# Moving the softmax's 1e-9 to GpSimd in ten units, with another opening order, one load of constants and a last product in two halves

## The chip, the core and the metric

The kernel runs on one core of one Trainium2 chip. A core has TensorE (PE, matrix products; its weight loads are listed as PEld), VectorE (DVE), ScalarE (ACT), GpSimd (POOL), and SyncE (SP), which here issues nearly all transfers. Each engine works through its own queue in order, and semaphores tie the queues together. The metric is the device time of one execution in microseconds.

## The reference

Eight batches of eight heads, 576 positions of 64 values. Heads 0 to 3 attend to the last 32 positions, heads 4 to 7 to every fourth of the last 128. The result, 4608 tokens of 512, goes through a layer with 1024 hidden values.

```python
scores = np.where(masks, scale * q @ k.T, -1e9)
attn = np.exp(scores - max(scores))
attn = attn / (np.sum(attn, axis=-1, keepdims=True) + 1e-09)
x = (attn @ v)                       # tokens x 512
h = x @ w_in                         # 512 -> 1024
e = np.exp(h - max(h)); sm = e / (sum(e) + 1e-9)
solu = h * sm
ln = (solu - mean(solu)) / np.sqrt(var(solu) + 1e-6) * g_ln
out = ln @ w_out                     # 1024 -> 512
```

The weights arrive as 64-bit floats and are turned into 32-bit ones on the chip. All products have 32-bit accuracy: each operand is split into a high and a low part, and three products of the parts are added.

## The kernel before, in words

There are 32 units (a batch and a pair of heads) and 36 tiles of 128 tokens. The order of every engine's queue is written out by hand: a list of words is run in order, and each word calls a function that issues its instructions to their engines. OPENING is the list for units 0 to 8 or so and tiles 0 to 5; STEP, PAIR and LAST_PAIR give the rest in loops.

A unit n goes through these words. `q` and `v` load its operands (lines 209, 210 and 217, on SP). `S` makes the scores on PE; in units 0 to 9 (PE_MASK) the mask is added by a product with the identity (line 247) ahead of the score products (line 255). `max` and `sub` find and subtract the maximum (DVE, lines 281 and 291; in the units of ACT_SCORES the scores are first copied out of PSUM by ACT, `cp`, line 285, and POOL subtracts, line 294). `exp` is ACT's (line 298), `sum` DVE's (line 302). `inv` adds 1e-9 and takes the reciprocal, both on DVE (lines 306 and 307). `norm` multiplies on POOL (line 312), `turn` transposes on DVE (line 317), `V` is the product with v on PE (line 333). `xh` and `xl` copy the result out as a high part (ACT, line 371) and a low part (DVE, line 388; in the units of POOL_X ACT makes a second copy, `xc`, line 375, and POOL subtracts, line 382).

The sixteen blocks of weights are loaded (`w`, line 232) and converted: `abs` and `low` on ACT (lines 780 and 790), `clamp`, `sign` and `join` on DVE (lines 796, 803 and 811), `gain` and `hi` on ACT (lines 818 and 821), `lo` on POOL, or on DVE for the blocks of DVE_LOW (line 825). In the first 88 us these fill the same queues as the softmax.

A tile i goes through `ha`, `hb`, `hc`, `hd` (a quarter each of the first product, line 401), `peak` (its row maximum, DVE, line 412), `e` (ACT, line 427), `gate` and `mid` (product, mean and centring, lines 436 to 445, with the centring on ACT in tiles 0 to 4), `var` (square and sum on ACT, line 452, then six small POOL operations that make rstd, lines 463 to 468), `forth` and `back` (through DRAM), `tr`, `th`, `tl` (transpose and split), `o` (the second product, line 531) and `out` (scaling and store, lines 544 to 555). Score and value products of a unit share PSUM banks with their neighbours: a unit's mask product waits until ACT or DVE has read the previous results there.

The last tile's output is scaled in two halves, by ACT (line 548) and DVE (line 551), into one tile, and each half is stored.

Of the kernel before, what the change touches and what calls it, by code (L numbers as in the profile page):

```python
# [130 lines left out]
def windowed_attention_then_solu_kernel(  # L131
# [7 lines left out]
    g_ln: bass.AP,  # L139
    mask: bass.AP,  # L140
    ident: bass.AP,
    ident_bf: bass.AP,
# [20 lines left out]
    id_sb = const.tile([P, P], F32, name="id_sb")  # L163
    mask_sb = const.tile([P, 2, NS * WQ], BF16, name="mask_sb")
    g_sb = const.tile([P, FT], F32, name="g_sb")
    id_bf = const.tile([P, P], BF16, name="id_bf")
# [137 lines left out]
    def soft_inv(n):  # L304
        rs = st[n]["rs"]
        nc.vector.tensor_scalar(out=rs, in0=rs, scalar1=1e-9, scalar2=None, op0=ALU.add)
        nc.vector.reciprocal(out=rs, in_=rs)
# [232 lines left out]
    def moe_out(i):  # L540
        ob = moe.tile([P, DO], F32, name="ob", bufs=1)
        rows, rstd = out[i * P : i * P + P, :], ms[i]["rstd"]
        if i < NTILE - 1:
            nc.scalar.activation(out=ob, in_=ps_o(i), func=AF.Copy, scale=rstd)  # L544
            nc.sync.dma_start(out=rows, in_=ob)
        else:
            left, right = slice(0, DO // 2), slice(DO // 2, DO)
            nc.scalar.activation(
                out=ob[:, left], in_=ps_o(i)[:, left], func=AF.Copy, scale=rstd
            )  # L550
            nc.vector.tensor_scalar(
                out=ob[:, right], in0=ps_o(i)[:, right], scalar1=rstd, scalar2=None, op0=ALU.mult
            )
            nc.scalar.dma_start(out=rows[:, left], in_=ob[:, left])
            nc.sync.dma_start(out=rows[:, right], in_=ob[:, right])
# [414 lines left out]
```

## Time and profile before

| what | value |
|---|---|
| runs | 501.33, 502.91, 503.94 us; median 502.91 |
| profiled execution | 504.69 us, of which the span of the trace is 502.8 |
| PE busy | 469.9 us (93%) |
| DVE, ACT, POOL busy | 351.4, 291.3, 298.7 us |
| transfers | 94.14 MB, mean 187 GB/s |

Busy time is the time in which an engine executes; a group's mean is that of one instruction. A wait is put down to what ended it. The chain of work that ended last is followed back from the last instruction, so it shows which engine set the end at each moment. "Issue" stands for idle time in which an engine waited for nothing that the profile shows. Times in the trace are counted from the start of the span.

### The profile page before, as it was taken

What the parts mean: (1) busy time and instruction counts of PE and PEld (TensorE: products, weight loads), DVE (VectorE), ACT (ScalarE), POOL (GpSimd) and SP (SyncE); (2) the same over time, 40 slices, a digit from 0 to 9 for tenths busy, and PEclk for the clock granted to TensorE, in tenths of its full rate; (3) what the DMA queues carried; (4) which work ended last, traced back from release to release, by engine and by line L of the source; (5) the groups of instructions that cost most, each with busy time, mean ns of one, the idle gap of its engine ahead of it and who ended that gap; (6) DMA issues with size and microseconds to landing.
All of it is one profiled execution on the core that took longest, in us unless ns stands there. A gap on an engine that the chain in (4) does not pass through costs nothing.

```text
span 502.8 us, 16542 instructions
## 1 busy us (share of the span) xinstructions
PE 469.9 (93%) x7064; PEld 376.0 (75%) x7064; DVE 351.4 (70%) x619; ACT 291.3 (58%) x483; POOL 298.7 (59%) x367
## 2 busy tenths in 40 slices
PE   1457998999999999999999999999999999999996
PEld 1336776788878888788878787878787888888875
DVE  3996989867627788777868686868676865445562
ACT  3766897744424444534457575757575767666551
POOL 1652776556533765778976666665756555766440
PEclk9999999999999999999999999999999999999999
DMA  7979175664465655666667677676765545354461
GB/s 280 402 254 359 37 261 163 230 190 133 137 193 156 194 164 169 186 175 178 201 175 216 206 211 211 210 211 211 212 210 164 160 129 146 104 168 124 113 188 63
DMA packets 51337, 94.14 MB, mean 187 GB/s; under 512 B 5952, under 2 KB 26048, under 8 KB 51264
## 3 DMA queue, kind: packets, MB, share of 16 engines
q1 hardware_dynamic: 50544, 92.43, 59.6%
q8 instruction: 55, 0.90, 0.8%
q10 hardware_dynamic: 720, 0.66, 0.4%
q14 instruction: 18, 0.15, 0.1%
HBM read 60.04 MB, written 28.31 MB: 176 GB/s over the span
## 4 chain that ended last, share of the span: by engine, by line
PE 91%; DMA 5%; issue 2%; DVE 1%; ACT 0%; SPq 0%; DVEq 0%; ACTq 0%
PE banks L531 40%; PE banks L733 20%; PE banks L401 18%; PE banks L333 7%; PE banks L255 6%; DMA qt<-qT 2%; DMA raw<-w_in 2%; DMA kt<-kT 1%; DVE pt L317 0%; PE banks L247 0%; DVE x_lo L388 0%; DVE nmax L412 0%; SPq L232 0%; DVE rs L302 0%; ACT sm L285 0%
## 5 line engine op out<-in xcount | busy, mean ns | idle before, releaser
L531 PE MATMUL banks<-w_o,th 128*128 128x512 f32 x576 | 179.9, 393 | 0.0
L522 POOL TENSOR_TENSOR tl<-t,th 128x512 fp32r<-128x512 f32 x68 | 87.9, 1305 | 59.9 <-ACT th L516 59.8
L531 PEld LDWEIGHTS banks<-w_o,th 128*128 128x128 f32 x576 | 106.6, 188 | 22.6 <-ACT th L516 0.6
L531 PE MATMUL banks<-w_o,tl 128*128 128x512 f32 x288 | 112.5, 391 | 0.0
L401 PE MATMUL banks<-w_i,x_hi 128*128 128x512 f32 x256 | 82.8, 405 | 0.2 <-DVE mu L436 0.2
L531 PEld LDWEIGHTS banks<-w_o,tl 128*128 128x128 f32 x288 | 54.0, 188 | 12.3 <-DVE tl L522 0.9
L516 ACT CAST th<-t 128x512 fp32r<-128x512 f32 x72 | 43.4, 621 | 23.5 <-DVE t L508 16.1
L401 PEld LDWEIGHTS banks<-w_i,x_hi 128*128 128x128 f32 x256 | 47.2, 191 | 11.1 <-DVE mu L436 0.8
L508 DVE STREAM_TRANSPOSE t<-raw 128x512 f32<-128x512 f32 x72 | 46.9, 684 | 6.1 <-DMA out<-ob 3.0
L401 PE MATMUL banks<-w_i,x_lo 128*128 128x512 f32 x128 | 50.7, 396 | 0.0
L333 PEld LDWEIGHTS banks<-pt,vt 32*64 32x64 f32 x2816 | 35.3, 138 | 20.0 <-issue 12.8
L452 ACT ACTIVATE e<-t 128x1024 f32<-128x1024 f32 x35 | 37.0, 1058 | 17.6 <-DVE t L448 17.3
L294 POOL TENSOR_TENSOR sm<-sm,mx 128x640 f32<-128x640 f32 x27 | 34.5, 1276 | 21.4 <-DVE mx L281 18.8
L333 PE MATMUL banks<-pt,vt 32*64 32x64 f32 (+3 forms) x2816 | 38.8, 234 | 8.6 <-issue 5.4
L298 ACT ACTIVATE sm<-sm 128x640 f32<-128x640 f32 x32 | 23.6, 739 | 35.8 <-POOL sm L294 35.1
L255 PEld LDWEIGHTS banks<-kt,qt 64*32 64x32 f32 x2560 | 29.8, 112 | 17.7 <-issue 10.7
L269 DVE TENSOR_TENSOR sm<-banks,mask_sb 128x640 f32<-128x640 f32 x22 | 18.1, 824 | 35.1 <-PE banks L255 35.0
L255 PE MATMUL banks<-kt,qt 64*32 64x64 f32 x2560 | 35.7, 238 | 5.6 <-issue 4.1
L544 ACT ACTIVATE ob<-banks,rstd 128x512 f32<-128x512 f32 x35 | 24.0, 686 | 24.8 <-issue 16.6
L757 DVE CUSTOM_DVE_ANT_0 t<-banks,t 128x512 f32<-128x512 f32 x30 | 20.7, 690 | 22.3 <-PE banks L733 16.9
L751 ACT COPY t<-banks 128x512 f32<-128x512 f32 x30 | 17.6, 588 | 30.3 <-PE banks L733 30.3
L427 ACT ACTIVATE e<-t,nmax 128x1024 f32<-128x1024 f32 x19 | 21.9, 1153 | 18.8 <-DVE nmax L764 18.2
(151 smaller groups left out, 868.5 us busy)
## 6 DMA issues: line engine op xcount, KB each, us to landing
mid<-t SPq DMA_DIRECT2D x140, 128.0 KB, 2.4
raw<-mid SPq DMA_DIRECT2D x34, 512.0 KB, 3.9
vt<-vw SPq DMA_DIRECT2D x32, 384.0 KB, 3.9
kt<-kT SPq DMA_DIRECT2D x32, 312.0 KB, 4.4
qt<-qT SPq DMA_DIRECT2D x32, 296.0 KB, 4.7
out<-ob SPq DMA_DIRECT2D x35, 256.0 KB, 2.7
x_hi<-x SPq DMA_DIRECT2D x12, 288.0 KB, 3.5
t<-w_in SPq DMA_DIRECT2D x5, 512.0 KB, 7.8
```

What stands on the lines that cost most here:

```text
L255: nc.tensor.matmul(out=ps[WIN * c : WIN * c + WIN, h, WQ * i : WQ * i + WQ], lhsT=qt[D * h : D * h + D, q0 : q0 + WIN], rhs=kt[D * h : D * ...
L294: eng.tensor_tensor(out=st[n]["sm"], in0=st[n]["sm"], in1=wide(mx), op=ALU.subtract)
L298: nc.scalar.activation(out=sm, in_=sm, func=AF.Exp, scale=0.125)
L333: nc.tensor.matmul(out=ps_x[D * h : D * h + D, c, c0 : c0 + k1 - k0], lhsT=vt[WIN * c : WIN * c + WIN, i, D * h : D * h + D], rhs=pt[WIN * ...
L401: nc.tensor.matmul(out=ps_h(i)[:, half], lhsT=a[:, kt, xs], rhs=w_i[:, kt, half, part, :], start=(kt == 0 and k == 0), stop=(kt == KT - 1 ...
L452: nc.scalar.activation(out=e, in_=t, func=AF.Square, accum_out=per_tile(i, "sq"))
L508: nc.vector.transpose(out=turned(i)[:, cut(c)].rearrange("p k (a r) -> p k a r", r=WIN), in_=ms[i]["mv"].rearrange("p (a k s) -> p k a s", ...
L516: nc.scalar.copy(out=ms[i]["th"][:, cut(c)], in_=turned(i)[:, cut(c)])
L522: eng.tensor_tensor(out=ms[i]["tl"][:, cut(c)], in0=turned(i)[:, cut(c)], in1=ms[i]["th"][:, cut(c)].bitcast(F32), op=ALU.subtract,)
L531: nc.tensor.matmul(out=ps_o(i), lhsT=a[:, f, :], rhs=w_o[:, f, part, :], start=(f == 0 and k == 0), stop=(f == FT - 1 and k == 2), skip_gr ...
L544: nc.scalar.activation(out=ob, in_=ps_o(i), func=AF.Copy, scale=rstd)
L733: nc.tensor.matmul(out=banks[:, bank], lhsT=left(pa, kt), rhs=right(pb, kt), start=j in (1, 2, 5) and kt == 0 and k == 0, stop=kt == 1 and ...
```

## The change

Four things. First, in units 0 to 9 the 1e-9 is added to the softmax's sum by POOL; the reciprocal stays on DVE, next in its queue after the sum. Second, OPENING is another order of nearly the same words, and with it three sets change: ACT_SCORES, POOL_X and DVE_LOW. Third, the identity, the masks and the gains come in one array with one transfer, `pack`, at the head of the list, in place of four transfers (a fifth, `i`, was not used). Fourth, the last tile's second product is made in two halves of 256 columns in two PSUM banks; the left half's output is scaled by ACT while the right half is multiplied, and the right half's output in two quarters, by ACT and DVE, into two tiles.

```diff
-ACT_SCORES = (1, 5, 7, 8, 9)
-POOL_X = (0, 4, 5)
-DVE_LOW = (12, 13, 14, 15)
+ACT_SCORES = (2, 5, 6)
+POOL_X = (4, 5)
+DVE_LOW = (13,)
...
-    "w1 ib abs1 w3 m0 low1 q0 clamp1 w0 sign1 w2 abs3 q1 low3 q2 join1 hi1 S0 sign3 clamp3 "
+    "pack q0 S0 w0 q1 max0 sub0 low0 abs0 w3 exp0 abs3 S1 q2 clamp0 low3 sign0 sum0 w2 inv0 "
...
+    "max6 cp6 exp5 low14 lo10 gate0 q10 mid0 hb1 sum5 sub6 V4 v8 var0 inv5 peak1 w13 e1 sign8 "
...
-    "oA.b oB.b out.b "
+    "oL.b outL.b oR.b outR.b "
...
     def soft_inv(n):
         rs = st[n]["rs"]
-        nc.vector.tensor_scalar(out=rs, in0=rs, scalar1=1e-9, scalar2=None, op0=ALU.add)
+        eng = nc.gpsimd if n in PE_MASK else nc.vector
+        eng.tensor_scalar(out=rs, in0=rs, scalar1=1e-9, scalar2=None, op0=ALU.add)
         nc.vector.reciprocal(out=rs, in_=rs)
...
+    def moe_o_half(i, half):
+        th, tl = ms[i]["th"], ms[i]["tl"]
+        cols = slice(DO // 2 * half, DO // 2 * half + DO // 2)
+        for f in range(FT):
+            for k, (a, part) in enumerate(((th, 0), (th, 1), (tl, 0))):
+                nc.tensor.matmul(
+                    out=banks[:, half, cols],
+                    lhsT=a[:, f, :],
+                    rhs=w_o[:, f, part, cols],
...
+    def moe_out_part(i, half, cols, on_act):
+        if half == 0:
+            ob = moe.tile([P, DO], F32, name="ob", bufs=1)
+        else:
+            ob = att.tile([P, 2, NS, WQ], F32, name=f"sm{int(on_act)}")
...
+        if on_act:
+            nc.scalar.activation(out=ob[:, cols], in_=ps[:, cols], func=AF.Copy, scale=rstd)
+            nc.scalar.dma_start(out=rows[:, cols], in_=ob[:, cols])
+        else:
+            nc.vector.tensor_scalar(
+                out=ob[:, cols], in0=ps[:, cols], scalar1=rstd, scalar2=None, op0=ALU.mult
+            )
+            nc.sync.dma_start(out=rows[:, cols], in_=ob[:, cols])
+
+    def out_left(i):
+        moe_out_part(i, 0, slice(0, DO // 2), True)
+
+    def out_right(i):
+        moe_out_part(i, 1, slice(DO // 2, DO * 3 // 4), True)
+        moe_out_part(i, 1, slice(DO * 3 // 4, DO), False)
...
+        "pack": lambda _: nc.sync.dma_start(out=packed, in_=pack),
```

How instructions move, at three places. First the start of SP's queue, the transfers up to unit 1's operands. Before:

```order
L232 DMA t_98<-w_in 128x1024
L833 DMA id_bf<-ident_bf 128x128
L232 DMA t_103<-w_in 128x1024
L835 DMA mask_sb<-mask 128x320
L209 DMA kt_109<-kT 128x624
L210 DMA qt_108<-qT 128x592
L232 DMA t_113<-w_in 128x1024
L232 DMA t_116<-w_in 128x1024
L209 DMA kt_121<-kT 128x624
L210 DMA qt_120<-qT 128x592
```

Now:

```order
L858 DMA packed<-pack 128x392
L206 DMA kt_97<-kT 128x624
L207 DMA qt_96<-qT 128x592
L229 DMA t_142<-w_in 128x1024
L206 DMA kt_145<-kT 128x624
L207 DMA qt_144<-qT 128x592
```

Unit 0's operands stand second and third in place of fifth and sixth, and one block of weights, not four, stands ahead of unit 1's.

Second, POOL's queue round unit 5's normalization (sm1_822 before, sm1_784 now) and tile 0's rstd (the names s2, sq and rstd). Before:

```order
L294 TENSOR_TENSOR sm1_822<-sm1_822,mx_812 128x640
L825 TENSOR_TENSOR w_o_87<-mag0_592,w_o_87 128x512
L825 TENSOR_TENSOR w_o_87<-mag1_687,w_o_87 128x512
L312 TENSOR_TENSOR sm1_822<-sm1_822,rs_887 128x640
L382 TENSOR_TENSOR x_lo_89<-x_904,x_hi_88 128x576
L825 TENSOR_TENSOR w_o_87<-mag2_690,w_o_87 128x512
L463 TENSOR_SCALAR se_892<-se_892 128x1
L464 TENSOR_TENSOR s2_1029<-se_892 128x1
L465 TENSOR_SCALAR s2_1029<-s2_1029 128x1
L466 TENSOR_SCALAR sq_1027<-sq_1027 128x1
L467 TENSOR_TENSOR s2_1029<-s2_1029,sq_1027 128x1
L468 TENSOR_TENSOR rstd_1030<-s2_1029,mhalf_84 128x1
```

Now:

```order
L291 TENSOR_TENSOR sm0_854<-sm0_854,mx_852 128x640
L461 TENSOR_SCALAR se_844<-se_844 128x1
L462 TENSOR_TENSOR s2_930<-se_844 128x1
L463 TENSOR_SCALAR s2_930<-s2_930 128x1
L464 TENSOR_SCALAR sq_928<-sq_928 128x1
L465 TENSOR_TENSOR s2_930<-s2_930,sq_928 128x1
L466 TENSOR_TENSOR rstd_931<-s2_930,mhalf_81 128x1
L304 TENSOR_SCALAR rs_875<-rs_875 128x10
L310 TENSOR_TENSOR sm1_784<-sm1_784,rs_875 128x640
```

Unit 5's multiplication stood ahead of tile 0's rstd; now it, and the new add ahead of it (line 304), stand behind.

Third, DVE's queue at the same place (rs_887 and rs_875 are unit 5's sum, mu_907 and mu_861 tile 0's mean, nmax_971 and nmax_940 tile 1's peak). Before:

```order
L302 TENSOR_REDUCE rs_887<-sm1_822 128x10
L803 TENSOR_SCALAR low2_881<-t3_746 128x512
L306 TENSOR_SCALAR rs_887<-rs_887 128x10
L307 RECIPROCAL rs_887<-rs_887 128x10
L436 ISA t0_906,mu_907<-banks_90,e_891 128x1024
L436 ISA mu_907 128x1
L444 TENSOR_SCALAR mu_907<-mu_907 128x1
L412 TENSOR_REDUCE nmax_971<-banks_90 128x1
```

Now:

```order
L434 ISA t0_860,mu_861<-banks_87,e_843 128x1024
L434 ISA mu_861 128x1
L442 TENSOR_SCALAR mu_861<-mu_861 128x1
L299 TENSOR_REDUCE rs_875<-sm1_784 128x10
L305 RECIPROCAL rs_875<-rs_875 128x10
L410 TENSOR_REDUCE nmax_940<-banks_87 128x1
```

Unit 5's sum moved behind tile 0's mean, its add is gone from DVE, and tile 1's peak stands behind its reciprocal. On ACT, tile 1's exponent, which needs that peak, stands in the new order ahead of unit 4's `xh`, unit 6's `exp` and unit 4's `xc`; before, unit 4's `xh` and `xc` stood ahead of tile 0's centring.

More of the change, by code (lines that the diff above doesn't have):

```diff
@@ L138, in windowed_attention_then_solu_kernel @@
     w_out: bass.AP,
[L139 to L142, printed above, removed]
+    pack: bass.AP,
     out: bass.AP,
@@ L161, in windowed_attention_then_solu_kernel @@
     )
[L163 to L166, printed above, removed]
+    packed = const.tile([P, P // 2 + NS * WQ + FT], F32, name="packed")
+    id_bf = packed[:, 0 : P // 2].bitcast(BF16)
+    mask_sb = packed[:, P // 2 : P // 2 + NS * WQ].bitcast(BF16).rearrange("p (d c) -> p d c", d=2)
+    g_sb = packed[:, P // 2 + NS * WQ :]
     mhalf = const.tile([P, 1], F32, name="mhalf")
@@ L542, in moe_out @@
         rows, rstd = out[i * P : i * P + P, :], ms[i]["rstd"]
-        if i < NTILE - 1:
-            nc.scalar.activation(out=ob, in_=ps_o(i), func=AF.Copy, scale=rstd)
-            nc.sync.dma_start(out=rows, in_=ob)
-        else:
-            left, right = slice(0, DO // 2), slice(DO // 2, DO)
-            nc.scalar.activation(
-                out=ob[:, left], in_=ps_o(i)[:, left], func=AF.Copy, scale=rstd
-            )
[L551 to L555, printed above, removed]
+        nc.scalar.activation(out=ob, in_=ps_o(i), func=AF.Copy, scale=rstd)
@@ new lines, in moe_out @@
+        nc.sync.dma_start(out=rows, in_=ob)
+        del ms[i]
+    def moe_o_half(i, half):
[7 more added lines that the diff above has]
+                    rhs=w_o[:, f, part, cols],
+                    start=(f == 0 and k == 0),
+                    stop=(f == FT - 1 and k == 2),
+                    skip_group_check=True,
+                )
@@ new lines, in moe_out_part @@
+    def moe_out_part(i, half, cols, on_act):
+        if half == 0:
+            ob = moe.tile([P, DO], F32, name="ob", bufs=1)
+        else:
+            ob = att.tile([P, 2, NS, WQ], F32, name=f"sm{int(on_act)}")
+            ob = ob.rearrange("p h s w -> p (h s w)")
+        rows, rstd = out[i * P : i * P + P, :], ms[i]["rstd"]
+        ps = banks[:, half]
+        if on_act:
[4 more added lines that the diff above has]
+                out=ob[:, cols], in0=ps[:, cols], scalar1=rstd, scalar2=None, op0=ALU.mult
+            )
+            nc.sync.dma_start(out=rows[:, cols], in_=ob[:, cols])
@@ L831, in windowed_attention_then_solu_kernel @@
         "q": load_qk, "v": load_v, "w": load_w,
-        "i": lambda _: nc.sync.dma_start(out=id_sb, in_=ident),
-        "ib": lambda _: nc.sync.dma_start(out=id_bf, in_=ident_bf),
-        "g": lambda _: nc.sync.dma_start(out=g_sb, in_=g_ln),
-        "m": lambda d: nc.sync.dma_start(out=mask_sb[:, d], in_=mask[:, d]),
+        "pack": lambda _: nc.sync.dma_start(out=packed, in_=pack),
         "abs": conv_abs, "low": conv_low, "clamp": conv_clamp, "sign": conv_sign,
@@ L849, in windowed_attention_then_solu_kernel @@
         "oA": lambda i: moe_o(i, range(FT // 2)), "oB": lambda i: moe_o(i, range(FT // 2, FT)),
+        "oL": lambda i: moe_o_half(i, 0), "oR": lambda i: moe_o_half(i, 1),
+        "outL": out_left, "outR": out_right,
         "xf": spread_hi, "xd": move_x, "pk": peak_of,
@@ L952 @@
         "w_out": _bits(_by_blocks(inputs["moe_w_out"]).reshape(DF, DO)),
-        "g_ln": np.ascontiguousarray(_by_blocks(inputs["moe_g_ln"]).reshape(FT, P).T),
-        "mask": _mask().astype(ml_dtypes.bfloat16),
-        "ident": np.eye(P, dtype=np.float32),
-        "ident_bf": np.eye(P, dtype=np.float32).astype(ml_dtypes.bfloat16),
+        "pack": np.concatenate(
+            [
+                np.eye(P, dtype=ml_dtypes.bfloat16).view(np.float32),
+                _mask().astype(ml_dtypes.bfloat16).reshape(P, -1).view(np.float32),
+                np.ascontiguousarray(_by_blocks(inputs["moe_g_ln"]).reshape(FT, P).T),
+            ],
+            axis=1,
+        ),
     }
```

47 rows, old and new, of the table OPENING are left out of this document.

## The prediction

> **What bounds the kernel now.** I read the page first, then a table of stretches, then PE's waits in the stretch that has any, then the busy groups of the engines behind those waits.
>
> The page's head, and its line on the queue that carries PE's instructions:
>
> ```profile
> span 502.8 us, 16542 instructions
> ...
> q8 instruction: 55, 0.90, 0.8%
> ```
>
> Stretches (start:end, length, then busy time and count of PE, PEld, DVE, ACT and POOL, clock, DMA share, GB/s):
>
> ```profile
> 0.00:10.00 10.00, 0.69 (x2) 0.21 (x2) 1.78 (x7) 4.21 (x7) 0.19 (x4) 1.00 0.73 247
> 10.00:40.00 30.00, 14.37 (x601) 10.54 (x602) 28.47 (x47) 18.77 (x31) 18.12 (x14) 1.00 0.93 337
> 40.00:88.00 48.00, 44.12 (x1041) 34.41 (x1040) 39.58 (x67) 38.65 (x62) 26.81 (x35) 1.00 0.60 197
> 88.00:250.00 162.00, 161.93 (x2384) 130.22 (x2372) 119.00 (x184) 73.58 (x123) 103.38 (x138) 1.00 0.59 178
> ```
>
> From 88 us on PE has no hole (161.93 of 162 us, and the same in the later stretches). Before that it is idle for 88 - 0.69 - 14.37 - 44.12 = 28.8 us. So the change can act in two places only: the opening, and the few microseconds behind the last product. In the opening, DVE is busy for 28.47 of the 30 us from 10 to 40: once data flows, DVE's queue sets the pace, and PE stands behind it. What PE waits for in the first 88 us (total, times, longest):
>
> ```profile
> PE banks L247 <- DMA mask_sb<-mask: 8.8, 1, 8.8
> PE banks L333 <- issue: 5.4, 2, 2.8
> ...
> PE banks L255 <- issue: 4.1, 2, 3.0
> ```
>
> "Issue" is time for which the profile names no releaser; it comes to 9.5 us here.
>
> **Part 1, the opening's list, the loads and the split of the work (no moved add yet).** The start: the first score product ran at 10.49 us, and the first transfer (w1, 0.52 MB) had landed at 4.53:
>
> ```profile
> 10.49 1.39 PE L255 MATMUL banks<-kt,qt 64*32 64x64 f32 x80 [0.97 <-DMA qt<-qT]
> ...
> 4.53 0.66 ACT L780 ACTIVATE mag<-t 128x512 f32<-128x512 f32 x1 [2.31 <-DMA t<-w_in]
> ```
>
> Now pack, k0 and q0 come first: 0.20 + 0.32 + 0.30 = 0.82 MB in place of 1.78 MB. At the 247 GB/s of the first 10 us the extra 0.30 MB over w1 lands 1.2 us after 4.53, so S0 starts near 5.9 us, 4.6 us earlier. How much of that reaches the end? DVE's queue decides. These are its groups in the first 88 us (count | busy, mean ns):
>
> ```profile
> L811 DVE SCALAR_TENSOR_TENSOR mag<-mag,low 128x512 int32<-128x512 int32 x15 | 12.8, 859 | 0.1
> L796 DVE TENSOR_SCALAR mag<-mag 128x512 f32<-128x512 f32 x16 | 7.9, 500 | 4.3 <-ACT mag L780 4.3
> L302 DVE TENSOR_REDUCE rs<-sm 128x10 f32<-128x640 f32 x8 | 6.5, 810 | 1.0 <-ACT sm L298 1.0
> ...
> L412 DVE TENSOR_REDUCE nmax<-banks 128x1 f32<-128x1024 f32 x4 | 4.9, 1223 | 1.9 <-PE banks L401 1.9
> L436 DVE CUSTOM_DVE_ANT_0 t<-banks,e 128x1024 f32<-128x1024 f32 x4 | 4.8, 1191 | 0.3 <-ACT e L427 0.3
> L291 DVE TENSOR_TENSOR sm<-banks,mx 128x640 f32<-128x640 f32 x5 | 4.1, 823 | 0.1
> L388 DVE TENSOR_TENSOR x_lo<-banks,x_hi 128x576 fp32r<-128x576 f32 x5 | 3.8, 753 | 5.1 <-ACT x_hi L371 5.1
> ...
> L306 DVE TENSOR_SCALAR rs<-rs 128x10 f32<-128x10 f32 x8 | 1.9, 233 | 0.1
> ```
>
> S9, the last score product ahead of the stretch without holes, waits in the new order for DVE to finish unit 8's subtraction. I counted DVE's rows up to that place in the new order against those that DVE had done by 86.5 us, when S9 ran before. Two joins less (-2 x 0.86), two clamps less (-2 x 0.50), one subtraction more (+0.82, ACT_SCORES), one x_lo more (+0.75, POOL_X), one peak more (+1.22): +0.1 us. So the split of work is even, and only idle time of DVE can differ. DVE's first reduction can start near 7.3 us (5.9 + 1.4 of scores), where before it had 1.6 us of work behind it at 9.92: a lead of 1.0 us, which one wait for ACT's first conversion (0.7 to 1.4 us) takes back. I take 0 for this part. Its ends: -4.6 if all of the earlier start lasts, +3.0 if one more PE stall as long as the longest "issue" row falls where PE had no slack. PE's first eight groups (S0 S1 S2 V0 S3 V1 S4 V2) stand in the same sequence in both lists, so I expect the "issue" holes to come at the same instructions again.
>
> [...]
>
> **Part 2, the 1e-9 on GpSimd.** DVE loses ten adds of 0.233 us. But the reciprocal follows in DVE's queue and now waits for POOL, with all of DVE's later work behind it. The price of a bare hop:
>
> ```profile
> 33.75 0.22 DVE L307 RECIPROCAL rs<-rs 128x10 f32<-128x10 f32 x1
> ...
> 34.11 1.51 POOL L312 TENSOR_TENSOR sm<-sm,rs 128x640 f32<-128x640 f32 x1 [0.94 <-DVE rs L307]
> ...
> 62.88 0.24 POOL L463 TENSOR_SCALAR se<-se 128x1 f32<-128x1 f32 x1
> ...
> 63.97 0.21 POOL L466 TENSOR_SCALAR sq<-sq 128x1 f32<-128x1 f32 x1
> ...
> 64.53 0.83 POOL L468 TENSOR_TENSOR rstd<-s,mhalf 128x1 f32<-128x1 f32 x1
> ```
>
> DVE ends at 33.97, POOL starts at 34.11: 0.14 over, 0.24 for the add (nearest row: POOL's TENSOR_SCALAR on one column), some 0.1 back: 0.48 of waiting less 0.233 saved = +0.25 a unit. Nine such hops are 2.3 us of DVE; only five fall where DVE is dense (1.2 us), and of those the start's lead and PE's own holes cover most. I take +0.4, ends 0 and 2.3.
>
> Unit 5 is not a bare hop. In the new POOL order its add stands behind the six small operations of tile 0's rstd, and these wait for ACT's centring and square of tile 0. ACT's rows of the same work before:
>
> ```profile
> 55.65 0.74 ACT L298 ACTIVATE sm<-sm 128x640 f32<-128x640 f32 x1 [0.17 <-POOL sm L294]
> 56.30 0.60 ACT L821 CAST w_o<-mag 128x512 fp32r<-128x512 f32 x1
> 56.81 1.11 ACT L427 ACTIVATE e<-banks,nmax 128x1024 f32<-128x1024 f32 x1
> ...
> 57.91 0.63 ACT L371 CAST x_hi<-banks 128x576 fp32r<-128x576 f32 x1
> 58.43 0.65 ACT L375 COPY x<-banks 128x576 f32<-128x576 f32 x1
> ...
> 60.05 1.15 ACT L445 ACTIVATE t<-t,mu 128x1024 f32<-128x1024 f32 x1 [0.40 <-DVE mu L444]
> 61.23 1.06 ACT L452 ACTIVATE e<-t 128x1024 f32<-128x1024 f32 x1
> ...
> 62.42 1.12 ACT L427 ACTIVATE e<-banks,nmax 128x1024 f32<-128x1024 f32 x1
> ```
>
> From tile 0's mean on, POOL's chain ends after 1.18 (centre, start to start) + 1.19 (square) + 1.39 (POOL, 63.97 to 65.36) = 3.8 us. DVE fills 0.81 + 0.14 of that with unit 5's sum, then stands: 2.8 us. Behind the reciprocal on DVE stands tile 1's peak; for that waits ACT's exponent of tile 1; behind that on ACT stand x_hi of unit 4, unit 6's exponent and the copy of unit 4's PSUM; and for that copy waits PE's S7. From the mean: 3.8 + 0.24 + 0.1 + reciprocal 0.22 + peak 1.22 + exponent 1.10 + 0.52 + 0.65 + 0.65 = 8.5 us. Tile 0's mean comes 1.22 + 1.10 + 1.19 + some 0.5 of hand-offs and the read-back = 4.0 us after PE's last product of tile 0, so S7 may start 12.5 us after that product. PE's own work in between, by the chain of work that ended last:
>
> ```profile
> 51.64 0.97 PE banks L255 x64
> 52.60 2.97 PE banks L401 x12
> 55.57 1.13 PE banks L333 x74
> ```
>
> S6 with its mask 1.26, half of tile 1 2.97, V4 1.13, tile 2 whole (24 products, twice 2.97 less a switch) about 5.7: 11.1 us, and more if S6 itself waits for its bank. So PE stands 0 to 1.4 us if DVE is on time, and up to 2.8, the whole hold, if DVE is late there, which its load makes likely. I take +1.5, ends 0 and 2.8. Without the hold (2.8 less) S7 would not wait: the move pays for it alone.
>
> Three lo's also move to POOL (DVE_LOW). They are due after 88 us, where POOL has over a third of its time free (103.38 of 162): nothing, or at most 3 x 1.5 us of lateness (the row at 34.11 is a longer pass) if that cover is gone.
>
> **Part 3, the last product and its output.** The end before, and PE's weight loads:
>
> ```profile
> 498.90 0.47 ACT L548 ACTIVATE ob<-banks,rstd 128x256 f32<-128x256 f32 x1 [5.02 <-PE banks L531]
> ...
> 499.47 0.48 DVE L551 TENSOR_SCALAR ob<-banks,rstd 128x256 f32<-128x256 f32 x1 [5.43 <-ACT ob L548]
> 499.98 0.33 SPq L555 DMA_DIRECT2D out<-ob x1
> ...
> 492.77 0.30 PEld L531 LDWEIGHTS banks<-w_o,th 128*128 128x128 f32 x2 [0.17 <-ACT th L516]
> ...
> L531 PEld LDWEIGHTS banks<-w_o,th 128*128 128x128 f32 x576 | 106.6, 188 | 22.6 <-ACT th L516 0.6
> ```
>
> ACT and DVE scaled their halves one after the other: 1.08 us from 498.90 to the last issue. Now the left half is done under the right half's products, and behind those stand two quarters in two tiles, side by side: about 0.4 us (0.47 for 256 columns is the upper bound). That saves 0.65; if they still go in turn, 0.2. Against it, 24 products of 512 columns become 48 of 256, each with a weight load. If the columns set the pace they cost the same. Two weight loads of 0.19 us in 0.30 us start 0.11 apart, which just fits under half of a product (5.7 / 24 / 2 = 0.12). I take +0.1, ends 0 and 48 x 0.19 - 5.7 = +3.4 if a load can't start before the last one's end. Part 3: -0.55.
>
> [...]
>
> **Sum.** 0 + 0.4 + 1.5 - 0.55 = +1.35 us. The profiled execution took 504.69 (span 502.8, 1.9 around it), so 506.0 for it; the median of the three runs is 502.91, so 504.3 in those terms.
>
> **Rivals.** *The earlier start lasts* (faster): S0's 4.6 us carry through, the transfers ahead of the data are fewer, and S7's hold is covered. For it: the largest single PE wait (8.8) was for a small transfer. Against it: DVE's 28.47 of 30. By two thirds to all of 4.6, with part 3: -3.6 to -5.1, so about 499. *The hold and a stall* (slower): unit 5's wait costs its whole 2.8, and one hole of 3.0 falls behind 42 us, since PE now meets V6, V7 and the S's closer together: 2.8 + 0.4 + 3.0 - 0.55 = +5.6, about 508. It decides from the point where DVE's peak of tile 1 comes over 2 us after tile 1's last product. *Weight loads bind the halves* (slower): +3.3 on the forecast, about 507.6. *Nothing moves*: DVE hides its waits in the idle time it has from 40 to 88 us (48 - 39.58 = 8.4 us): 0.4 - 0.55, about 502.8.
>
> **How the numbers follow.** Forecast 0.42, nothing moves 0.14, start lasts 0.18, hold and stall 0.20, halves 0.06. A difference of 0.5% (2.5 us) is about what a measurement of this kernel can tell from no change. Forecast and "nothing moves" lie within it save for 0.04 on the slow side and 0.01 on the fast one; hence faster 0.19, same 0.51, slower 0.30. The range leaves out the far half of the fast and of the slow cases: 499.8 to 508.0.
>
> **What would show it.** Right: S0 near 6 us; DVE's reciprocals waiting for POOL's rs, one of them 2 us or more at about 55 to 62 us; S7's mask product waiting for ACT behind it; the last two scalings side by side. Wrong: no wait of DVE for POOL's rs over 1 us; "issue" holes under 5 us in all; PE without holes well before 82 us; 48 last products in over 6 us.

## The result and the profile after

The changed kernel took 508.67 us in the median of its first four executions (506.99 to 511.24) against 502.98 of the kernel before; the ratio is 1.0131, 95% interval 1.0087 to 1.0175. Six more executions, taken with the last experiments, gave 507.14 us (505.36 to 508.41), ratio 1.0082 (1.0052 to 1.0111). All ten together have a mean of 507.7 us, and 83 executions of the kernel before a mean of 502.8 us: 4.9 us slower, give or take 1.2. One execution of all the runs below counts as slow (508.35 us, in the run with operands early, add on DVE and extra products); it is in that run's median and left out of the differences. The forecast was 504.3 us, with "within 0.5%" as the likeliest.

The profiled execution took 506.99 us, 2.3 us more than that of before. It is the shortest of the first four, and that of before was longer than the median there, so the rows below account for about half of the 4.9 us. Its head, and the stretches that the prediction showed (start:end, length, busy time and count of PE, PEld, DVE, ACT and POOL, clock, DMA share, GB/s):

```profile
span 505.2 us, 16590 instructions
```

```profile
0.00:10.00 10.00, 2.11 (x82) 1.42 (x83) 1.25 (x5) 2.21 (x4) 0.19 (x4) 1.00 0.77 246
10.00:40.00 30.00, 16.69 (x613) 12.79 (x613) 26.96 (x43) 19.86 (x33) 15.32 (x15) 1.00 0.96 360
40.00:88.00 48.00, 39.71 (x870) 30.79 (x869) 38.26 (x63) 36.58 (x60) 28.84 (x44) 0.93 0.60 197
88.00:250.00 162.00, 162.00 (x2444) 130.51 (x2443) 117.84 (x181) 74.35 (x125) 101.65 (x134) 0.99 0.58 173
```

PE's idle time up to 88 us hardly changed (29.5 us in place of 28.8), but it moved: 3.7 us less of it before 40 us, 4.4 us more behind. And the clock column, 1.00 everywhere before, reads 0.93 and 0.99. PE's waits in the first 100 us (total, times, longest):

```profile
PE banks L244 <- DVE sm L288: 10.7, 4, 3.7
...
PE banks L244 <- DMA packed<-pack: 3.4, 1, 3.4
PE banks L252 <- DMA qt<-qT: 3.3, 1, 3.3
...
PE banks L331 <- issue: 1.7, 2, 1.3
```

The wait of 8.8 us for the mask is 3.4 for the packed constants, and the "issue" holes went from 9.5 to 1.9 us (the 1.7 shown and one of 0.2). DVE's subtraction and its other results took their place. Now PE itself, at the places that matter (start, duration, line, operation, and in brackets the idle time ahead of it and what ended it):

```profile
7.40 1.40 PE L252 MATMUL banks<-kt,qt 64*32 64x64 f32 x80 [3.32 <-DMA qt<-qT]
...
33.54 0.69 PE L244 MATMUL banks<-packed 128*128 128x320 bf16 x2 [3.37 <-DVE sm L288]
...
36.93 0.73 PE L399 MATMUL banks<-w_i,x_hi 128*128 128x512 f32 x2
...
62.99 0.43 PE L244 MATMUL banks<-packed 128*128 128x320 bf16 x2 [1.40 <-ACT x L373]
...
73.66 0.30 PE L331 MATMUL banks<-pt,vt 32*64 32x16 f32 x8 [1.30 <-issue]
75.51 1.48 PE L331 MATMUL banks<-pt,vt 32*64 32x64 f32 x80 [1.54 <-DVE x_lo L386]
77.09 1.22 PE L399 MATMUL banks<-w_i,x_hi 128*128 128x512 f32 x2
...
87.79 0.48 PE L244 MATMUL banks<-packed 128*128 128x320 bf16 x2 [1.77 <-DVE sm L288]
...
107.01 1.20 PE L331 MATMUL banks<-pt,vt 32*64 32x32 f32 x96
```

S0 runs 3.1 us earlier than before (7.40, not 10.49), and tile 0's first product 5.9 us earlier. Before, that product was the first of these rows; the second is S8, and the last V8, the one at 107.01 above:

```profile
42.84 1.22 PE L401 MATMUL banks<-w_i,x_hi 128*128 128x512 f32 x2
...
77.62 0.43 PE L247 MATMUL banks<-mask_sb,id_bf 128*128 128x320 bf16 x2 [1.70 <-DVE x_lo L388]
...
104.97 1.20 PE L333 MATMUL banks<-pt,vt 32*64 32x32 f32 x96
```

So the lead was there at 37 us, and it was lost between 41 and 96 us. The holes at S7 (62.99), in V6 (73.66), ahead of V7 (75.51) and of S9 (87.79), with two more at 42.7 and 50.4 us (1.4 and 0.8), come to 8.2 us where before had 2.4 (one of 1.70 and two of 0.5 and 0.2). The rest is the clock. The same stretch in pieces:

```profile
74.00:76.00 2.00, 0.49 (x33) 0.49 (x34) 0.96 (x2) 1.98 (x4) 1.75 (x4) 0.60 1.09 358
76.00:78.00 2.00, 1.90 (x70) 1.70 (x59) 2.00 (x5) 2.00 (x4) 1.68 (x5) 0.50 0.90 287
78.00:80.00 2.00, 2.00 (x6) 1.52 (x6) 1.81 (x5) 2.00 (x3) 0.60 (x3) 0.50 0.95 272
80.00:82.00 2.00, 2.00 (x8) 1.57 (x7) 1.66 (x4) 1.97 (x6) 1.49 (x4) 0.69 0.54 190
...
88.00:90.00 2.00, 2.00 (x83) 1.63 (x82) 1.97 (x5) 1.76 (x3) 0.00 (x0) 0.51 0.51 162
90.00:92.00 2.00, 2.00 (x7) 1.52 (x7) 1.97 (x5) 1.42 (x3) 0.00 (x0) 0.63 1.01 328
```

Read as time at 1.00 and time at 0.50, the rows say that PE is granted half its clock from 74.4 to 81.2 us and again from 88.0 to 91.5 us: 6.8 and 3.4 us. In the chain of waits the 24 products of tile 4 and of tile 5 take 7.68 and 6.59 us in place of the usual 5.69:

```profile
77.09 7.68 PE banks L399 x24
...
89.61 6.59 PE banks L399 x24
...
108.20 5.69 PE banks L399 x24
```

That is 2.0 + 0.9 us, and V7 and S9 cost 0.4 each: 3.7 us that no wait shows. In the prediction's own view of before the clock was 1.00 in every stretch, and its hole of 1.70 us had left no mark.

S9 itself, behind the same work of PE in both orders, came only 1.0 us late (87.79 us, not 86.77). Its hole can be read from the two lists. Unit 8 was in ACT_SCORES before: ACT copied its scores out of PSUM right behind S8, and S9 waited for nothing. Now DVE's subtraction has to release the bank, and the list puts tile 4's peak and unit 8's maximum ahead of it, so DVE first waits for PE's tile 4 and then PE for DVE. The ACT row of before, and the DVE rows of now:

```profile
79.06 0.69 ACT L285 COPY sm<-banks 128x640 f32<-128x640 f32 x1 [0.74 <-PE banks L255]
```

```profile
84.80 1.23 DVE L410 TENSOR_REDUCE nmax<-banks 128x1 f32<-128x1024 f32 x1 [3.15 <-PE banks L399]
86.06 0.82 DVE L278 TENSOR_REDUCE mx<-banks 128x10 f32<-128x640 f32 x1
86.92 0.82 DVE L288 TENSOR_TENSOR sm<-banks,mx 128x640 f32<-128x640 f32 x1
```

The opening's lead (5.9), and 1.5 more for before's first nine products of tile 0, which ran slow (3.7 us for what takes 2.2 in the changed kernel), less the holes (8.2 - 2.4 = 5.8) and the half clock (3.7) makes 2.1 us of loss. The rows show 2.0: V8 stands behind the same work in both and runs at 107.01 in place of 104.97. At the last tile's second product the difference is 2.3 us, so little comes in between.

### The profile page after: what moved, and what is told of

The parts are those of the page before. It is cut to its first block, busy times and chain, and to the rows that moved or that the text cites. A ratio compares the mean times of both kernels' runs of the same rounds, so it can differ in the third digit from the quotient of the medians.

```text
span 505.2 us, 16590 instructions
## 1 busy us (share of the span) xinstructions
PE 471.9 (93%) x7088; PEld 379.4 (75%) x7088; DVE 348.6 (69%) x609; ACT 289.3 (57%) x481; POOL 297.2 (59%) x377
## 4 chain that ended last, share of the span: by engine, by line
PE 83%; DVE 7%; ACT 3%; issue 2%; DMA 2%; POOL 2%; SPq 0%; DVEq 0%; ACTq 0%
PE banks L529 36%; PE banks L759 20%; PE banks L399 15%; PE banks L331 6%; PE banks L252 5%; DMA t<-w_in 1%; PE banks L550 1%; DVE mx L278 1%; DVE low L829 1%; POOL w_i L851 1%; DVE mag L837 1%; DVE mag L822 1%; DVE t L434 1%; DMA mid<-t 1%; ACT low L816 1%
## 5 line engine op out<-in xcount | busy, mean ns | idle before, releaser
L529 PE MATMUL banks<-w_o,th 128*128 128x512 f32 x560 | 175.1, 394 | 0.0
L529 PEld LDWEIGHTS banks<-w_o,th 128*128 128x128 f32 x560 | 103.7, 188 | 21.7 <-ACT th L514 0.4
L520 POOL TENSOR_TENSOR tl<-t,th 128x512 fp32r<-128x512 f32 x68 | 88.5, 1315 | 50.6 <-ACT th L514 50.4
L529 PE MATMUL banks<-w_o,tl 128*128 128x512 f32 x280 | 109.2, 390 | 0.0
L399 PE MATMUL banks<-w_i,x_hi 128*128 128x512 f32 x256 | 83.9, 410 | 0.1
L529 PEld LDWEIGHTS banks<-w_o,tl 128*128 128x128 f32 x280 | 52.6, 188 | 11.6 <-DVE tl L520 0.4
L514 ACT CAST th<-t 128x512 fp32r<-128x512 f32 x72 | 43.5, 620 | 28.8 <-DVE t L506 15.0
L266 DVE TENSOR_TENSOR sm<-banks,packed 128x640 f32<-128x640 f32 x22 | 18.1, 823 | 39.3 <-PE banks L252 39.3
L291 POOL TENSOR_TENSOR sm<-sm,mx 128x640 f32<-128x640 f32 x25 | 31.5, 1261 | 22.4 <-DVE mx L278 16.9
```

The source lines that it names most:

```text
L291: eng.tensor_tensor(out=st[n]["sm"], in0=st[n]["sm"], in1=wide(mx), op=ALU.subtract)
L399: nc.tensor.matmul(out=ps_h(i)[:, half], lhsT=a[:, kt, xs], rhs=w_i[:, kt, half, part, :], start=(kt == 0 and k == 0), stop=(kt == KT - 1 ...
L514: nc.scalar.copy(out=ms[i]["th"][:, cut(c)], in_=turned(i)[:, cut(c)])
L520: eng.tensor_tensor(out=ms[i]["tl"][:, cut(c)], in0=turned(i)[:, cut(c)], in1=ms[i]["th"][:, cut(c)].bitcast(F32), op=ALU.subtract,)
L529: nc.tensor.matmul(out=ps_o(i), lhsT=a[:, f, :], rhs=w_o[:, f, part, :], start=(f == 0 and k == 0), stop=(f == FT - 1 and k == 2), skip_gr ...
```

## The experiments

Each time is a median; "lost clock" is (1 - mean granted clock) times the span, averaged over a kernel's executions. It was 5.7 us in the first four of the changed kernel and 2.9 in the other six, and 1.2 in those of before. Differences between kernels are between means, with twice their standard error. The runs below were made on four chips, on which the kernel before had means of 502.3 to 503.2 us; a difference between runs of two chips carries up to 0.9 us more.

### The add back on DVE, under the new list and taken to the old one

```diff
-        eng = nc.gpsimd if n in PE_MASK else nc.vector
+        eng = nc.vector
```

> The changed kernel with the 1e-9 added on DVE in every unit again; the rest of the change stays. Theory A (the add's hold): unit 5's add behind tile 0's rstd puts DVE some 2.8 us back at 58 us, this makes the holes of 1.3 to 1.8 us in PE at 72 to 88 us, and behind those holes the granted clock falls to a half for some 8 us in all, which costs 3.7 us. Then S7's mask product no longer waits for ACT (1.4 us gone), the clock stays near 1.00 in 74 to 92 us, and the time is 500.5 to 503.5, ratio to before 0.995 to 1.001. Theory B (the list): the holes ahead of V6, V7 and S9 come from the new list's order, whichever engine adds. Then S7's wait may go, but the clock falls to a half in 74 to 92 us all the same, and the time is 505 to 508, ratio 1.005 to 1.012.

Measured: 507.03 us, ratio 1.0083 (1.0055 to 1.0112), lost clock 4.4. Nearly all of the slowdown is still there without the moved add: 0.7 ± 1.3 us under the ten executions of the changed kernel. So theory B, the list, carries most. S7's wait shows why the hold's end brought so little:

```profile
62.72 0.45 PE L244 MATMUL banks<-packed 128*128 128x320 bf16 x2
64.53 1.03 PE L252 MATMUL banks<-kt,qt 64*32 64x64 f32 x80 [1.36 <-DMA qt<-qT]
```

The mask product no longer waits for ACT (1.40 before), but the score products right behind it now wait 1.36 us for unit 7's operands. A hidden wait as long as the first stood behind it. The holes ahead of V7 and S9 do not depend on the engine of the add: they are 1.54 to 1.70 and 1.77 to 1.78 us in all seven profiles of the new list in which S8 and PE's products are as in the change.

The other way round, the kernel before with only the add on POOL:

```diff
-        nc.vector.tensor_scalar(out=rs, in0=rs, scalar1=1e-9, ...)
+        (nc.gpsimd if n in PE_MASK else nc.vector).tensor_scalar(out=rs, in0=rs, scalar1=1e-9, ...)
```

> The kernel before with one edit: the 1e-9 is added by POOL in units 0 to 9, under the old list. There unit 5's multiplication stands ahead of tile 0's rstd on POOL, so its add is a bare hop like the others, unless POOL has joins queued there. Theory A (the hold behind the rstd is what costs): ten hops of about 0.15 to 0.25 us net on DVE, mostly covered: 502.5 to 505, ratio 0.999 to 1.004, no wait of DVE for POOL's rs over 1.5 us. Theory B (the list): the same, 502.5 to 505. Theory D (the add costs on POOL wherever it stands, since POOL's queue is full in the opening and the reciprocal waits behind joins): 506 to 508, ratio 1.006 or more, with several waits of DVE for POOL's rs over 1.5 us.

Measured: 506.85 us, ratio 1.0074 (1.0044 to 1.0103), lost clock 4.0. Both A and B fall here, and D is nearest: under a list that was not laid out for it, the same add costs 4.0 ± 0.7 us. The reciprocals of units 6 and 7 are the ones that wait long; on POOL unit 6's add stands behind the six small operations of a tile's rstd (66.58 to 68.63 us), unit 7's behind a `lo` of 1.28 us:

```profile
69.03 0.22 DVE L307 RECIPROCAL rs<-rs 128x10 f32<-128x10 f32 x1 [2.09 <-POOL rs L306]
78.46 0.22 DVE L307 RECIPROCAL rs<-rs 128x10 f32<-128x10 f32 x1 [1.46 <-POOL rs L306]
```

Under the new list again, with unit 5's add alone back on DVE:

```diff
+        eng = nc.gpsimd if n in PE_MASK and n != 5 else nc.vector
```

> The changed kernel with the add back on DVE in unit 5 alone; nine units still add on POOL. Theory A (the hold of unit 5): all that the add costs goes with this one unit: the time is that of the run with every add on DVE within 1 us, and S7's wait for ACT is gone. Theory D (the hops cost too): it stays at least 1.5 us above the run with every add on DVE. Theory B (the list): 505 to 508 with the clock at a half in 74 to 92 us.

Measured: 508.51 us, ratio 1.0106 (1.0074 to 1.0137). Unit 5's hold alone, taken away, gains nothing (0.7 ± 1.2 us over the changed kernel): S7 waits 1.62 us for the same operands. It lies 1.4 ± 0.8 us above the run with every add on DVE.

### The rest of the change under the old list

The change with the old OPENING and its three sets, the packed load in the place of the first small one, and the add on DVE:

```diff
-ACT_SCORES = (2, 5, 6)
+ACT_SCORES = (1, 5, 7, 8, 9)
...
-    "pack q0 S0 w0 q1 max0 sub0 low0 abs0 w3 exp0 abs3 S1 q2 clamp0 low3 sign0 sum0 w2 inv0 "
+    "w1 pack abs1 w3 low1 q0 clamp1 w0 sign1 w2 abs3 q1 low3 q2 join1 hi1 S0 sign3 clamp3 "
```

> The changed kernel with the old opening list and its three sets (constants in the one packed load, put at the place of the first small load), and the add on DVE: what is left of the change is the packed load and the last product in halves with its quarters of output. By the forecast's part 3 (-0.55) and the mask arriving with the first constants: 501.5 to 503, ratio 0.997 to 1.000. If the halves cost what their loads bind (48 products in over 6 us): 503 to 506. Theories A and B both say that the clock stays near 1.00 in 74 to 92 us here.

Measured: 503.18 us, ratio 1.0006 (0.9979 to 1.0032). The packed load and the halved last product change nothing that can be told. The new list is then the difference between this run and the one with the add on DVE: 3.6 ± 1.2 us. Its order and its three sets were never run apart, so which of the two costs what is not shown.

### S8 moved

```diff
-V6 var2 xh6 e3 low12 xl6 gate3 V7 ... xl7 ... S8 ... max8 sub8
+V6 var2 xh6 e3 low12 xl6 gate3 S8 V7 max8 ... xl7 sub8
```

> The changed kernel with one thing moved: S8 stands between V6 and V7 on PE (not next to S9), its maximum right behind on DVE and its subtraction behind unit 7's x_lo. Two pairs that share a bank, V6 with V7 and S8 with S9, then no longer stand side by side; the add stays on POOL. Theory B (the list's neighbours make the holes, the holes halve the clock): the holes of 1.5 us ahead of V7 and of 1.8 us ahead of S9 go, the half-clock stretches go with them or become one, and the time falls from 508.7 to 503 to 505.5. Theory A (the hold of the add sets DVE back, whatever PE's order): the holes move elsewhere in 60 to 92 us, and the time stays at 507 to 509.

> The run with S8 moved, and the add back on DVE in all units. If the list's neighbours and the add's hold both make holes: 501 to 503.5, below the kernel before. If the add costs only by way of the clock, which S8's move mends already: the same as the run with S8 moved, within 0.7 us. Theory A: 502 or less, 5 us under the run with S8 moved.

Measured: 512.91 us (ratio 1.0202, 1.0169 to 1.0236) and, with the add on DVE, 510.97 (1.0196, 1.0157 to 1.0236). A miss: 4.6 ± 1.9 and 4.7 ± 1.9 us slower than the same without the move. The holes did not go, they moved and grew. PE in the first of the two:

```profile
74.68 0.30 PE L331 MATMUL banks<-pt,vt 32*64 32x16 f32 x8 [1.52 <-issue]
76.53 0.69 PE L244 MATMUL banks<-packed 128*128 128x320 bf16 x2 [1.54 <-DVE x_lo L386]
...
81.95 0.95 PE L331 MATMUL banks<-pt,vt 32*64 32x64 f32 x42 [2.48 <-issue]
95.20 1.03 PE L399 MATMUL banks<-w_i,x_hi 128*128 128x512 f32 x2 [2.68 <-DVE mu L434]
```

S8 itself waited for x_lo, which reads the same banks; with three groups of many small products in a row there was a second "issue" hole of 2.48 us inside V7; and tile 5 then waited 2.68 us for DVE's pass over tile 4, which S9 and its wait had covered. The neighbours V6-V7 and S8-S9 cannot be parted that simply: behind tile 4 PE has nothing else to do in this order.

### Keeping PE busy in the holes

Extra products into PSUM that nothing reads, ahead of V7 and of S9, first into spare columns of a bank that other engines read then:

```diff
+    def keep_warm(k):
+        for _ in range(k):
+            nc.tensor.matmul(out=banks[:, 4, GQ : GQ + NS * WQ], lhsT=id_bf, rhs=mask_sb[:, 0, :], ...)
...
-gate3 V7
+gate3 wk6 V7
...
-S9
+wk7 S9
```

> The changed kernel with 6 extra products of 320 columns ahead of V7 and 7 ahead of S9, written to PSUM columns that nothing reads: PE works through its two largest holes and waits for the same releases as before. Clock theory: PE's granted clock no longer falls to a half behind these holes, mean loss of granted time falls from 5.7 us to under 2, and the time to 504.5 to 506. If the clock only follows and the waits for DVE set the end in any case: 508 to 510, the same holes and no gain. If the extra products outlast the holes: 509 to 511.

> The run with the extra products, and the add back on DVE in all units. Clock theory with the add's own delay (hold 1.4 us at S7): 503 to 505, 1 to 2 us under the run with the extra products and the add on POOL. If the add costs by way of the clock alone: within 0.7 us of it.

Measured: 509.07 us (1.0141, 1.0115 to 1.0168) and 507.79 (1.0124, 1.0093 to 1.0155); lost clock 2.4 and 2.5. Inconclusive: the lost clock fell by two fifths (4.1 in all ten of the changed kernel, 4.4 with the add on DVE), but the first group of extra products waited for x_lo itself and then ran slow on PE's path, six in 1.76 us where the seven ahead of S9 took 1.12:

```profile
76.70 1.76 PE L858 MATMUL banks<-packed 128*128 128x320 bf16 x6 [1.54 <-DVE x_lo L386]
```

So their 1.76 us were paid in full. The next try wrote to a bank that was free:

```diff
+            nc.tensor.matmul(out=banks[:, 1], lhsT=id_bf, rhs=packed[:, P // 2 : P // 2 + 256].bitcast(BF16), ...)
...
+gate3 wk4 V7
+wk6 S9
```

> The changed kernel with 4 extra products of 512 columns ahead of V7 and 6 ahead of S9, this time into a bank that no engine reads or writes then, so that they wait for nothing (the first try's waited for x_lo like V7 itself, as its profile shows: 1.54 us of waiting ahead of the extra products). Clock theory: the waits for x_lo and for the subtraction end when they did, PE is busy in them, the loss of granted time falls from 5.7 to under 3 us, and the time from 508.7 to 505 to 507. If waits for DVE set the end in any case: the loss falls, and the time stays at 508 to 509.5. If they fail to fill the holes in time: no change in either.

Measured: 506.75 us, ratio 1.0084 (1.0055 to 1.0112), lost clock 2.8. Now they ran inside the holes (0.57 and 0.37 us of waiting were left of 1.54 and 1.77):

```profile
75.34 1.04 PE L858 MATMUL banks<-packed 128*128 128x512 bf16 x4
76.95 1.48 PE L331 MATMUL banks<-pt,vt 32*64 32x64 f32 x80 [0.57 <-DVE x_lo L386]
87.70 1.47 PE L858 MATMUL banks<-packed 128*128 128x512 bf16 x6
89.55 0.43 PE L244 MATMUL banks<-packed 128*128 128x320 bf16 x2 [0.37 <-DVE sm L288]
```

Against the first four executions of the changed kernel this is 1.7 ± 2.3 us better, against all ten 0.6 ± 1.7: the mean doesn't settle it. Its own six executions nearly line up by their clock: 505.45 us at 1.000, 505.95 at 0.997, 506.58 at 0.995, 506.91 at 0.993, 509.15 at 0.992 and 508.87 at 0.990.

### Unit 7's operands earlier in SP's queue

```diff
-gate0 q10 mid0 ... w13 e1 sign8 q7
+gate0 q7 q10 mid0 ... w13 e1 sign8
```

> The changed kernel with unit 7's operands asked for ahead of unit 10's in SP's queue (there unit 10's wait for S6, and v8 for V4, with unit 7's behind them); the add stays on POOL. With the add moved back, S7 waited for these operands in place of ACT's copy. Theory A+ (the hold of unit 5 and the late operands end S7's wait at the same place, each hides the other): with the add on POOL the hold alone still ends S7's wait, so no gain here: 508 to 509. Theory Q (the operands alone): 506.5 to 507.5.

> The same with the add on DVE in all units. Theory A+: now both are gone, S7 starts without a wait, 1.1 to 1.5 us under the run with the add on DVE alone (507.0): 505.5 to 506, and some more if half-clock stretches go. If later waits take it back: 507 as without it.

Measured: 508.12 us with the add on POOL (ratio 1.0100, 1.0075 to 1.0125), 505.77 with the add on DVE (1.0047, 1.0022 to 1.0072). As theory A+ had it: nothing gained while unit 5's hold is there (S7 still waits 1.75 us, which the profile puts down to a transfer, while ACT's late copy ends at the same time; without the hold the wait is gone), and 1.6 ± 1.2 us gained once the hold is gone. SP's queue shows what held these operands: ahead of them SP waits 4.9 us for S6 (unit 10's kt) and 3.2 for V4 (unit 8's v). With the add on DVE and the old place, and then with the new one (issues of kt, each with its qt right behind; unit 7's is at 58.07 and then at 46.92, unit 10's the other):

```profile
53.13 0.33 SPq L206 DMA_DIRECT2D kt<-kT  x1
...
58.07 0.42 SPq L206 DMA_DIRECT2D kt<-kT  x1
```

```profile
46.92 0.42 SPq L206 DMA_DIRECT2D kt<-kT  x1
...
51.89 0.33 SPq L206 DMA_DIRECT2D kt<-kT  x1
```

The same list with only unit 5's add on DVE:

```diff
-gate0 q10 mid0 ... w13 e1 sign8 q7
+gate0 q7 q10 mid0 ... w13 e1 sign8
...
+        eng = nc.gpsimd if n in PE_MASK and n != 5 else nc.vector
```

> The changed kernel with unit 7's operands asked for ahead of unit 10's, and unit 5's add alone back on DVE. With these operands early, the two runs with the add on POOL and on DVE lay 2.35 us apart (508.1 and 505.8). If the hold of unit 5 makes up most of this: 505.5 to 506.5. If the nine bare hops do: 507.3 to 508.3. By the forecast's terms (hold 1.5, hops 0.4): 506.2.

Measured: 505.35 us, ratio 1.0046 (1.0020 to 1.0073). With the operands early, unit 5's add alone makes the whole difference between 508.1 and 505.4: the hold costs 3.0 ± 1.3 us there (2.7 by the two ratios to the kernel before), and the nine bare hops nothing that can be told (-0.4 ± 1.5). In both runs S7 starts without a wait.

And the list with the early operands, the add on DVE and the extra products in the free bank:

```diff
-gate0 q10 mid0 ... w13 e1 sign8 q7 ... gate3 V7 ... S9
+gate0 q7 q10 mid0 ... w13 e1 sign8 ... gate3 wk4 V7 ... wk6 S9
```

> The same again with the 4 and 6 extra products that wait for nothing. If the new list's cost over the old one (some 3.9 us) is S7's wait, the half clock and the rest of PE's holes in that order: 503 to 505. If the holes move and stay as long: 506 to 508.

Measured: 505.43 us (1.0037, 1.0010 to 1.0063), lost clock 1.3 in place of 3.3. The clock was better and the time hardly so (0.7 ± 1.6); 2.0 ± 1.3 us of the new list remain over the old one with extra products.

### The clock under the old list

```diff
-xl6 lo11 gain12 S8
+xl6 lo11 gain12 wk6 S8
```

> The old opening list under the rest of the change, add on DVE (503.2 when run alone), with 6 extra products that wait for nothing ahead of S8, whose wait for x_lo (1.5 us) was PE's longest hole behind 40 us there. Clock theory: the loss of granted time goes from 1.3 us to under 0.5 and the time to 502 to 502.8. It would be the fastest so far, if by less than a measurement tells. If the extra products outlast the hole: 503.5 or more.

Measured: 502.24 us, ratio 1.0003 (0.9985 to 1.0021); lost clock 0.1, so nine in ten of the half clock went. It is the fastest kernel of the study with the rest of the change in it, and level with the kernel before: nothing here beats that one by an amount that can be told.

The same with the add on POOL, and extra products ahead of V6 as well:

```diff
-        eng = nc.vector
+        eng = nc.gpsimd if n in PE_MASK else nc.vector
...
-turn6 sub7 V6
+turn6 sub7 wk6 V6
```

> The old list with the add on POOL (506.9 in its own run with before's ending and loads), with 6 extra products that wait for nothing ahead of V6 and 6 ahead of S8, the rest of the change kept. If the add's price there (3.9 us) is paid by way of the half clock: 503.5 to 504.5. If it is DVE's late reciprocals of units 6 and 7 (2.1 and 1.5 us of waiting for POOL) that delay what the end waits for: 506 to 507.5 with the loss under 2 us.

Measured: 505.31 us, ratio 1.0051 (1.0034 to 1.0069), lost clock 0.4. Between the two expectations: 1.5 ± 0.8 us under the run with the add on POOL and no extra products (which had 4.0 us of lost clock, and before's ending and loads), and still 2.6 ± 0.8 over the one above. Its DVE waits for POOL's sums behind 40 us, and PE's wait for the DVE pass that stands behind the second of them (0.18 us with the add on DVE):

```profile
DVE rs L305 <- POOL rs L304: 3.6, 2, 2.1
```

```profile
80.50 0.73 PE L399 MATMUL banks<-w_i,x_hi 128*128 128x512 f32 x2 [1.38 <-DVE mu L434]
```

So about two thirds of the add's price under the old list remain when nearly no clock is lost. That these are the lateness of the two reciprocals, and the other third the clock that PE lost in waiting for them, fits the rows and is not shown.

At last the changed kernel once more, with no edit:

> The changed kernel itself once more, beside the others on one chip, for a firm base: 508 to 509.5 by its four executions so far (506.99 to 511.24), with 5 to 6 us of granted time lost.

Measured: 507.14 us, ratio 1.0082 (1.0052 to 1.0111), lost clock 2.9. Lower than expected; the numbers above count both samples.

Over all 221 executions, with a level of its own for each kernel, an execution was 0.54 ± 0.14 us longer for each microsecond of lost clock. Where the clock goes is not the same in each execution of one kernel, which is much of their spread. For the change this makes 2.8 us of extra lost clock, so about 1.5 of the 4.9 us (an estimate, from that slope).

## Why the prediction was wrong

**Part 1, the list: the step that failed.** It was taken as 0, with ends -4.6 and +3.0; measured it is +3.6 ± 1.2. The working counted DVE's rows up to S9, found +0.1 us, and concluded that only DVE's idle time could differ. The count was right to half a microsecond: up to S9 DVE worked 66.3 us in the changed kernel and 68.6 before, and the eight adds moved by then (1.9 us) make up most of the difference. The step that failed is to take DVE's idle time as equal: it was 21.5 us in place of 18.2, with two new waits in it, 3.63 us for unit 5's add and 3.15 for tile 4. With the add on DVE, new list against old, it was 20.0 in place of 18.0. Behind 40 us PE doesn't follow DVE's amount of work but a chain of hand-overs: a product, a release by ACT or DVE, the next product in the same bank, and transfers that stand in a queue.

Three links were in the new list to be read: unit 7's operands behind two transfers that wait for S6 and V4 (1.6 us, shown by moving them), V7 right behind V6, and S9 right behind S8 with the subtraction on DVE between them (1.54 and 1.77 us of waiting, seen in the profile; not shown as a price, since the try to part them only moved the holes). Of these two only the second is new: before, S8 stood behind V6 and waited 1.70 us for the same x_lo. What makes up the other 2 us of the list's cost stays open.

The rival *the hold and a stall* named V6, V7 and the S's closer together and gave it 0.20; it came nearest, 508, though by another route. *The earlier start lasts* was right as far as 37 us, where tile 0's first product was 5.9 us ahead. S0 came at 7.40, not 5.9 us, and the "issue" holes, which were expected at the same instructions again, shrank to 1.9 us: a sign that the prediction had named as one against it, in the kernel's favour. By the counts of the rows two of before's four stand at the same instructions now, behind PE's 349th and 476th product, with 0.2 and 0.4 us in place of 3.0 and 2.6; the two behind the 222nd and the 603rd are gone.

**A term that was missing: PE's clock.** The sum knew of holes but not of what follows them. The granted clock fell to a half behind holes of 1.3 to 1.8 us and took 3.7 us in the profiled execution. A hole of 1.77 us alone stands ahead of the second fall, and one of 1.30 us with the next just begun ahead of the first; but the hole of 1.70 us in before's profile passed without a fall, and the run with extra products in the free bank lost 0 to 5.1 us of clock in its six executions. What decides whether the clock falls is not shown.

**Part 2, the add.** Unit 5's hold was where the prediction put it: DVE waited 3.63 us for POOL (2.8 was forecast), and S7 1.40 us (1.5 was forecast).

```profile
58.65 0.22 DVE L305 RECIPROCAL rs<-rs 128x10 f32<-128x10 f32 x1 [3.63 <-POOL rs L304]
```

But as a price it was wrong twice: in the kernel as it stands the add costs only 0.7 ± 1.3 us, not 1.9, since S7 would have waited for its operands anyway; with these early the hold costs 3.0 ± 1.3, more than the 1.4 us at S7, and the clock went with it (5.2 us lost with the hold, 2.9 without). The working asked what hides a cost, and not what is late next where a stall goes. The bare hops cost 0.36 to 0.40 us each where nothing is queued ahead of them on POOL, near the forecast (0.48); whether they cost the end anything stays open: +1.4 ± 0.8 us with the late operands, -0.4 ± 1.5 with the early ones.

**Part 3, the end.** Forecast -0.55; in the profiled pair it comes to +0.1. The output's tail is 0.44 us shorter (from the end of PE's last product to the end of the span: 3.54 us in place of 3.98), but not by working side by side, a sign that failed. The two quarters still go in turn, DVE 0.10 us behind ACT's end, though they now write two tiles:

```profile
501.69 0.37 ACT L568 ACTIVATE sm<-banks,rstd 128x128 f32<-128x128 f32 x1 [2.35 <-PE banks L550]
...
502.16 0.35 DVE L571 TENSOR_SCALAR sm<-banks,rstd 128x128 f32<-128x128 f32 x1 [5.74 <-ACT sm L568]
```

From ACT's start to the last issue it is 0.85 us in place of 1.08, the 0.2 that the prediction gave for this case; the rest of the 0.44 is mostly the time behind that issue (2.66 us in place of 2.82). Why DVE waits for ACT is not shown. Against it, the last tile's second product took 0.55 us longer, 6.51 us in place of 5.96 (first and last row of each, now and before):

```profile
495.15 0.51 PE L550 MATMUL banks<-w_o,th 128*128 128x256 f32 x2
...
501.38 0.28 PE L550 MATMUL banks<-w_o,tl 128*128 128x256 f32 x1
```

```profile
492.86 0.64 PE L531 MATMUL banks<-w_o,th 128*128 128x512 f32 x2
...
498.43 0.39 PE L531 MATMUL banks<-w_o,tl 128*128 128x512 f32 x1
```

About half of this is a longer wait for the low part in the first products. The rest is the halves: three take 0.36 us where three whole ones took 0.68 to 0.70, so 0.2 to 0.3 us in all where 0.1 was taken. The loads start 0.12 us apart and don't wait for one another's 0.19, as forecast; but "over 6 us" was a sign against the forecast, and it came. In the whole kernel this part can't be told from nothing (ratio 1.0006).

**The range** ended at 508.0, 0.7 us under the first median and 0.9 over the second one. It was made from the costs that the rows showed, one at a time, and left no room for holes that bring a slower clock with them.

## What to carry to other kernels

Where an engine works in a chain of hand-overs, compare two orders link by link: which product waits for whose release, and which transfer stands behind a waiting one. The busy time of the engine in between says little (DVE's up to S9 was 66.3 us in the slower kernel and 68.6 in the faster one). Before a wait is given a price, ask what is late next at the same place: two waits that end together hide each other, and either one alone looks free (S7's 1.40 us for ACT, and 1.36 for its operands once that was gone). And a hole in PE can cost more than itself: here the granted clock fell to 0.50 behind holes of 1.3 to 1.8 us, and 24 products took 7.68 and 6.59 us in place of 5.69. Look at the granted clock and at the length of the same product on both sides of the hole.
